# Top-k attention with a max-out MLP: the first sweep in seven groups of keys instead of eight

## The chip, the cores and the metric

The kernel runs on one core of one Trainium2 chip. The metric is device time in microseconds, the median of three runs. Five engines are named as the profile names them: PE (TensorE, its weight loads PEld), DVE (VectorE), ACT (ScalarE), POOL (GpSimd) and SP (SyncE, which issues the transfers).

## The reference

Eight batches of eight heads; 576 queries and 576 keys of 64 numbers each. Of each row of scores the 32 largest are kept, the rest are masked, then softmax and the product with the values. The heads are joined into 512 columns and go through a max-out MLP.

```python
scores = scale * np.matmul(q, k.transpose(0, 1, 3, 2))
kth = np.partition(scores, -top_k, axis=-1)[..., -top_k:-top_k + 1]
mask = scores >= kth
scores = np.where(mask, scores, -1000000000.0)
...
attn = attn / (np.sum(attn, axis=-1, keepdims=True) + 1e-09)
return np.matmul(attn, v).astype(np.float32)
...
h = np.maximum(np.maximum(x @ w1, x @ w2), x @ w3)
return (h @ w_out).astype(np.float32)
```

## The kernel before

**Tiles and units.** A tile is 128 queries (rows) of one head against all 576 keys. Two heads lie together, and a unit is mostly one pair of heads and two blocks of 128 queries, so four tiles; the last 64 queries of two pairs make a unit of two tiles. That is 80 units, ten to a batch, and 288 tiles. What follows happens per unit.

**Scores.** `qk` (L461, PE) multiplies queries and keys in two halves of 288 keys; `evac` (L469, ACT) moves each half from PSUM to the tile `ssb`.

**The search for the 32nd largest.** It has a rough and an exact step. `sweep` (L478, DVE) takes with MAX8 the eight largest, sorted, of each of eight groups of 72 keys: four groups after the first half of the scores has come, four after the second. The first four of each group (32 values, A) are negated by `negate` (L484, ACT) into `nA`; the last four (32 values, B) go to `pivot` piece 1 (L492, DVE), which keeps their eight largest in `b9`, behind a slot that holds a huge constant. Pieces 2 and 3 (L496, L502, L504) take the sixteen smallest of A in two MAX8 of `nA` with a MATCH_REPLACE8 between them; L498 gives the row's maximum. Piece 4 (L507) forms the minimum of A's (24-j)th largest and B's jth largest, for j = 0 to 7, and piece 5 (L509) the largest of these: the 24th largest of A and B together. This is the pivot. It is at most the true 24th largest of the row; its rank is 24 plus what the groups left out.

The exact step is `sign` (L517, ACT), which counts keys against the pivot, `window` (L522, POOL), which leaves the keys below the pivot positive, and `below` (L526, DVE), a MAX8 over all 576 that gives the next eight. `pick` (L537 to L542) chooses the 32nd by the count. This works while the pivot's rank is 24 to 32. `review` notes rows where it was not, and at the end a flag starts a second, slow pass over everything (the `tc.If(redo != 0)` block) if there is one.

**Softmax and values.** `mask` (L565, DVE), `expo` (L574, ACT), `inverse` (L589, DVE), `turn` (L620 to L625, PE transposes) and `turned` (L633, ACT), `values` (L650, PE), `scaled_x` (L667, DVE).

**MLP.** `layer` (L706, PE, three fp16 products for each of three weights), `largest` (L715, DVE, two of three; L713, ACT, the first), `high_h` and `low_h` (ACT, POOL), `layer2` (L766, PE). A batch's MLP needs all of its units. During the first batch VectorE also decodes the weights (L253 to L255).

**What sets the order.** Every engine works through its instructions in program order. `in_order` writes that order out: it lists the pieces of all units and the MLP, and picks, engine by engine, the piece that can start first by its own table of costs. Attention pieces are ranked by their unit plus a number from `OFFSETS`, within `LEAD` units of the lowest rank; `PATIENCE` says how long an engine may hold out for a piece of lower rank. The MLP is `fill`: PE takes it where no attention piece can start. So the costs and the tables decide where each instruction stands, on all engines.

Of the kernel before, what the change touches and what calls it, by code (L numbers as in the profile page):

```python
# [8 lines left out]
F32 = mybir.dt.float32  # L9
# [5 lines left out]
ALU = mybir.AluOpType  # L15
# [2 lines left out]
TOPK = 32  # L18
H_SCALE = 2.0 ** -12
CUT = 256  # L20
G = 8
GW = 72
NW = 9
SHRINK = 2.0 ** -61
BIG = 3.0e38
# [39 lines left out]
def in_order(pieces, fill):  # L65
# [72 lines left out]
DECODE_OUT = 1920.0  # L138
LOAD_JOB = 6500
SCORES = 960  # L140
PATIENCE = {'PE': 83.0, 'DVE': 164.4, 'ACT': 0.0, 'POOL': 81.9, 'SP': 0.0}


@with_exitstack
def kernel(ctx, tc, q, k, v, moe_w1, moe_w2, moe_w3, moe_w_out, out):
    nc = tc.nc
    B, NP, _, S = q.shape
    H, D = 2 * NP, q.shape[2] // 2
    P = 128
# [13 lines left out]
    sm = ctx.enter_context(tc.tile_pool(name="sm", bufs=3))  # L163
# [263 lines left out]
    b9s = [const.tile([P, 4, 9], F32, name=f"b9_{i}") for i in range(3)]  # L427
# [20 lines left out]
    def qk(n, g, i):  # L448


        b, hps, us = units[n]
        if n not in st:
            open_unit(n)
        s = ps_s.tile([P, 2, 512], F32, name="s")
        u = us[g]
        for x, hp in enumerate(hps):
            both = T_of[b, hp]
            c0, m, to = (u * P, P, s) if u < NU else (MAIN, 64, s[64 * x:64 * x + 64])
            for h in range(2):
                sl = slice(64 * h, 64 * h + 64)  # L460
                nc.tensor.matmul(to[:, h, :HALF], both[sl, 0, c0:c0 + m], both[sl, 1, i * HALF:(i + 1) * HALF], start=True, stop=True)  # L461
        st[n]["s"][g, i] = s

    def evac(n, g, i):
        d = st[n]
        if i == 0:
            t = d["both", g] = wk.tile([P, 2, S], F32, name="ssb", bufs=NSSB)
            d["ssb"] += [t[:, 0], t[:, 1]]
        nc.scalar.activation(d["both", g][:, :, i * HALF:(i + 1) * HALF], d["s"].pop((g, i))[:, :, :HALF], AF.Copy, scale=SCORE_SCALE)  # L469

    def sweep(n, g, i):

        d = st[n]
        if (g, i) == (0, 0):
            d["L"] = sm.tile([P, 4, G, 8], F32, name="L", bufs=NSM)
        for t in (2 * g, 2 * g + 1):
            for k in range(i * G // 2, (i + 1) * G // 2):
                nc.vector.max(d["L"][:, t, k, :], d["ssb"][t][:, k * GW:(k + 1) * GW])  # L478

    def negate(n):  # L480

        d = st[n]
        nA = d["nA"] = sm.tile([P, 4, G, 4], F32, name="nA", bufs=NSM)
        nc.scalar.activation(nA[:, :d["nt"]], d["L"][:, :d["nt"], :, 0:4], AF.Copy, scale=-1.0 / SHRINK)  # L484

    def pivot(n, piece):

        d = st[n]
        nt, L, nA = d["nt"], d["L"], d.get("nA")
        if piece == 1:  # L490
            for t in range(nt):
                nc.vector.max(b9s[n % 3][:, t, 1:9], L[:, t, :, 4:8])  # L492
        elif piece == 2:
            n8 = d["n8"] = sm.tile([P, 4, 2, 8], F32, name="n8", bufs=NSM)
            for t in range(nt):
# [330 lines left out]
    n = len(units)  # L826
# [10 lines left out]
    def attention(n):  # L837

        b, hps, us = units[n]
        nt = 2 * len(us)  # L840
        half = us[0] == NU
        gs = range(len(us))
        d = of[n] = {}
        p = lambda key, *a, **kw: d.setdefault(key, piece(*a, rank=(place_of[n], ("_" if b == 0 else "") + (key if isinstance(key, str) else "".join(map(str, key)))), **kw))
# [17 lines left out]
        swept = d["s", gs[-1], 1]
# [20 lines left out]
        for t in range(nt):  # L883
            g = t // 2
# [46 lines left out]
    def held(n, *key):  # L931
        return holders.setdefault((n, *key), [])
# [77 lines left out]
    with tc.If(redo != 0):  # L1010
        with tc.For_i(0, B, 1) as b:
# [79 lines left out]
```

## Time and profile before

| | us |
|---|---|
| median of three runs | 1258.01 (1257.69 to 1258.57) |
| the profiled execution | 1259.42 |
| its span, first to last instruction | 1257.6 |
| PE busy in the span | 1146.8 (91%) |
| DVE busy | 1146.7 (91%) |
| ACT busy | 1038.8 (83%) |
| POOL busy | 569.3 (45%) |
| PE weight loads busy | 776.2 (62%) |

How to read it: an engine's busy time is the union of its instructions, and two instructions in a row may overlap, since one starts before the last has left the engine. What an instruction costs its engine is therefore the distance from its start to the next one's, not its length. A busy share is an average over a startup, a long middle and a tail, which have different limits. The chain of waits is followed back from the last instruction; each step goes to what released it, or to the instruction before it.

### The profile page before, as it was taken

Reading aid. Unit: us, or ns where it says so; the run is one execution under the profiler, and the core shown is the slowest. Engines: PE = TensorE matmul, PEld = TensorE weight load, DVE = VectorE, ACT = ScalarE, POOL = GpSimd, SP = SyncE. Lnnn points to the kernel's source line nnn. Section 1 sums busy time; section 2 is a strip of 40 time slices with the busy share of each in tenths; the row PEclk is TensorE's granted clock in tenths of the full one; section 3 lists DMA queues with packets and bytes.
Section 4 is the critical chain, followed back from the end, with each engine's and each line's share of the span. In section 5 each row is a group of like instructions: output and inputs, shape, how many; then the busy total and the mean of one; then the engine's idle time right before and its main releaser. Section 6 shows DMA issues by size and latency. Waiting matters only on the chain.

```text
span 1257.6 us, 27583 instructions
## 1 busy us (share of the span) xinstructions
PE 1146.8 (91%) x8817; PEld 776.2 (62%) x8817; DVE 1146.7 (91%) x5728; ACT 1038.8 (83%) x2692; POOL 569.3 (45%) x503
## 2 busy tenths in 40 slices
PE   5275886999899999999999999999999999999998
PEld 2142653566576666766676666766677665767765
DVE  7999999999999999999999999999999999997121
ACT  6587888999989988999999989898899989897211
POOL 2444644654345544545555545445535454544111
PEclk8567986999999999999999999999999999999999
DMA  7141121202010102010101102020101000000000
GB/s 246 34 158 39 52 70 49 66 2 80 21 58 18 60 1 76 11 47 31 47 31 39 39 2 85 1 77 2 60 19 60 18 20 26 1 19 2 17 18 29
DMA packets 25754, 54.41 MB, mean 43 GB/s; under 512 B 2688, under 2 KB 2944, under 8 KB 25600
## 3 DMA queue, kind: packets, MB, share of 16 engines
q1 hardware_dynamic: 25296, 52.14, 12.6%
q8 instruction: 71, 1.16, 0.4%
q14 instruction: 83, 0.68, 0.2%
q10 hardware_dynamic: 304, 0.43, 0.1%
HBM read 43.12 MB, written 9.44 MB: 42 GB/s over the span
## 4 chain that ended last, share of the span: by engine, by line
DVE 49%; PE 39%; ACT 7%; issue 3%; POOL 1%; DMA 0%; ACTq 0%; DVEq 0%
PE m L706 19%; DVE L L478 13%; DVE ssb L565 9%; DVE Q L526 8%; PE m L766 5%; PE tr L625 5%; PE tr L650 5%; PE s L461 4%; DVE h L715 3%; DVE nR L502 2%; ACT w L517 2%; ACT pm L574 2%; DVE wall L254 1%; DVE n L504 1%; DVE n L496 1%
## 5 line engine op out<-in xcount | busy, mean ns | idle before, releaser
L522 POOL TENSOR_TENSOR w<-ssb,w 128x576 f32<-128x576 f32 x288 | 414.9, 1460 | 259.3 <-ACT w L517 257.0
L706 PE MATMUL m<-xh,wall 128*128 128x256 f16 (+1 forms) x2304 | 436.5, 287 | 4.8 <-DVE h L715 3.6
L706 PEld LDWEIGHTS <-wall 128*128 128x128 f16 x3456 | 338.0, 98 | 95.4 <-issue 15.9
L478 DVE MAX8 L<-ssb 128x8 f32<-128x72 f32 x2304 | 331.2, 218 | 6.8 <-ACT ssb L469 6.7
L706 PE MATMUL m<-xl,wall 128*128 128x320 f16 (+1 forms) x1152 | 330.7, 287 | 0.0
L574 ACT ACTIVATE pm<-ssb,nb 128x576 f32<-128x576 f32 x288 | 222.7, 775 | 42.4 <-DVE ssb L565 41.7
L565 DVE SCALAR_TENSOR_TENSOR ssb<-ssb,kth 128x576 f32<-128x576 f32 x288 | 241.7, 873 | 2.2
L517 ACT ACTIVATE w<-ssb,Q 128x576 f32<-128x576 f32 x288 | 223.2, 775 | 14.9 <-DVE Q L509 13.5
L633 ACT COPY pT<-tr 128x512 f32<-128x512 f32 (+1 forms) x432 | 215.1, 512 | 12.1 <-PE tr L622 6.6
L526 DVE MAX8 Q<-w 128x8 f32<-128x576 f32 x288 | 212.3, 747 | 1.3 <-POOL w L522 0.8
L625 PE MATMUL tr<-ident,pm 128*128 128x128 f32 x1152 | 183.0, 286 | 33.3 <-ACT pm L574 15.1
L461 PE MATMUL s<-qk 64*128 64x288 f32 (+1 forms) x1280 | 191.1, 451 | 16.6 <-ACT ssb L469 11.1
L469 ACT ACTIVATE ssb<-s 128x576 f32<-128x576 f32 x288 | 184.3, 650 | 10.0 <-PE s L461 9.7
L625 PEld LDWEIGHTS tr<-ident,pm 128*128 128x128 f32 x1152 | 130.2, 144 | 98.5 <-ACT pm L574 39.3
L650 PE MATMUL tr<-pT,vt 128*64 128x256 f32 (+1 forms) x1920 | 183.3, 340 | 0.1
L715 DVE SCALAR_TENSOR_TENSOR h<-m,rises,h 128x256 f32<-128x256 f32 (+1 forms) x192 | 97.2, 506 | 67.4 <-PE m L706 67.3
L650 PEld LDWEIGHTS tr<-pT,vt 128*64 128x64 f32 x1920 | 109.8, 140 | 69.1 <-issue 20.7
L721 POOL TENSOR_TENSOR hl<-h,hh 128x256 f16<-128x256 f32 (+1 forms) x96 | 72.7, 758 | 171.4 <-ACT hh L718 171.3
L461 PEld LDWEIGHTS s<-qk 64*128 64x128 f32 (+1 forms) x1280 | 99.9, 184 | 76.4 <-ACT ssb L469 28.2
L674 POOL TENSOR_TENSOR xl<-xs,xh 128x256 f16<-128x256 f32 (+1 forms) x80 | 55.1, 688 | 196.4 <-ACT xh L670 196.3
L766 PE MATMUL m<-wall,hh 128*128 128x512 f16 (+1 forms) x444 | 130.6, 377 | 3.2 <-ACT wall L318 1.2
L718 ACT CAST hh<-h 128x256 f16<-128x256 f32 (+1 forms) x96 | 41.5, 432 | 54.1 <-DVE h L715 53.4
(95 smaller groups left out, 1148.5 us busy)
## 6 DMA issues: line engine op xcount, KB each, us to landing
vt<-in_v_dram SPq DMA_DIRECT2D x32, 320.0 KB, 3.2
qk<-in_k_dram SPq DMA_DIRECT2D x34, 288.0 KB, 3.0
qk<-in_q_dram SPq DMA_DIRECT2D x33, 288.0 KB, 3.5
wall<-in_moe_w_dram SPq DMA_DIRECT2D x16, 512.0 KB, 6.0
out_dram<-ob SPq DMA_DIRECT2D x32, 256.0 KB, 2.0
wall<-in_moe_w_out_dram SPq DMA_DIRECT2D x3, 512.0 KB, 3.5
ssb<-in_moe_w_out_dram SPq DMA_DIRECT2D x3, 512.0 KB, 3.6
wall<-in_moe_w_dram SPq DMA_DIRECT2D x4, 256.0 KB, 5.9
```

Source lines behind the costliest of these rows:

```text
L461: nc.tensor.matmul(to[:, h, :HALF], both[sl, 0, c0:c0 + m], both[sl, 1, i * HALF:(i + 1) * HALF], start=True, stop=True)
L478: nc.vector.max(d["L"][:, t, k, :], d["ssb"][t][:, k * GW:(k + 1) * GW])
L517: nc.scalar.activation(d["w"][t], d["ssb"][t], AF.Sign, bias=d["Q"][:, t, 0:1], scale=-1.0, accum_out=d["cnt"][:, t:t + 1])
L522: nc.gpsimd.tensor_tensor(d["w"][t], d["ssb"][t], d["w"][t], ALU.mult)
L526: nc.vector.max(d["Q"][:, t, 1:NW], d["w"].pop(t))
L565: nc.vector.scalar_tensor_tensor(ss, ss, d["kth"][:, t:t + 1], ss, ALU.is_lt, ALU.subtract, accum_out=d["lost"][:, t:t + 1])
L574: nc.scalar.activation(d["pm", t // 2][:, t % 2], d["ssb"][t], AF.Exp, bias=d["nb"][:, t:t + 1], scale=-1.0 / SHRINK, accum_out=d["sums"][ ...
L625: nc.tensor.transpose(pt[:, j * P:(j + 1) * P], pm[:, i, 64 * i + j * P:64 * i + (j + 1) * P], ident)
L633: nc.scalar.copy(pT[:, 512 * i:512 * i + m] if i < 2 else pT[:, 8 * P:10 * P], pt[:, :m])
L650: nc.tensor.matmul(to, vt[:, block if i < 4 else 8 + h, :], keys, start=(i == 0), stop=(i == 4))
L706: nc.tensor.matmul(box["ps", i][:, :c1 - c0], a, bb[:, kc, c0:c1], start=(kc == 0 and k == 0), stop=(kc == KC - 1 and k == 2))
L766: nc.tensor.matmul(box["po"][:n, :ds.stop - ds.start], a[:, f, cs], columns_of(bb, ds), start=(f == 0 and k == 0), stop=(f == FC - 1 and k ...
```

## The change

The first sweep goes over seven groups of 82 or 83 keys (edges 0, 82, 164, 247, 329, 412, 494, 576). Three groups (up to key 247) are taken after the first half of the scores, four after the second, so a pair of tiles has 6 and then 8 MAX8, where it had 8 and 8. A and B have 28 values each. The 24th largest of A and B is now formed of nine pairs, j = 0 to 8: the slice `low` picks the 5th to the 13th of the sixteen smallest of A, and `b9` is used with all nine slots. The order's costs follow (890 and 1170 for the two halves, 1080 and 1080 before), and `LEAD`, `OFFSETS` and `PATIENCE` have new numbers, so that instructions stand elsewhere on all engines.

```diff
-G = 8
-GW = 72
+G = 7
+EDGES = (0, 82, 164, 247, 329, 412, 494, 576)
+FRONT = 3
...
-LEAD = 122.6
+LEAD = 121.4
...
-PATIENCE = {'PE': 83.0, 'DVE': 164.4, 'ACT': 0.0, 'POOL': 81.9, 'SP': 0.0}
+PATIENCE = {'PE': 102.7, 'DVE': 167.3, 'ACT': 0.0, 'POOL': 142.3, 'SP': 0.0}
...
-            for k in range(i * G // 2, (i + 1) * G // 2):
-                nc.vector.max(d["L"][:, t, k, :], d["ssb"][t][:, k * GW:(k + 1) * GW])
+            for k in range(FRONT, G) if i else range(FRONT):
+                nc.vector.max(d["L"][:, t, k, :], d["ssb"][t][:, EDGES[k]:EDGES[k + 1]])
...
-            z = d["z"] = sm.tile([P, 4, 8], F32, name="z", bufs=2)
-            nc.vector.scalar_tensor_tensor(z[:, :nt], d["n8"][:, :nt, 1], -SHRINK, b9s[n % 3][:, :nt, 0:8], ALU.mult, ALU.min)
+            z = d["z"] = sm.tile([P, 4, 9], F32, name="z", bufs=2)
+            low = d["n8"].rearrange("p t a b -> p t (a b)")[:, :nt, 4 * G - 24:4 * G - 15]
+            nc.vector.scalar_tensor_tensor(z[:, :nt], low, -SHRINK, b9s[n % 3][:, :nt], ALU.mult, ALU.min)
...
-                p(("s", g, i), "DVE", 1080, lambda g=g, i=i: sweep(n, g, i),
+                p(("s", g, i), "DVE", 1170 if i else 890, lambda g=g, i=i: sweep(n, g, i),
```

The line numbers of the changed kernel are one or two higher from here on (L478 is L479, L526 is L528, L650 is L652, L706 is L708).

**VectorE at the start of the program** (L is the tile of the group maxima, b the eight of B, nA the negated A, n the sixteen smallest; a row with a count stands for so many in a row). Before:

```order
L478 MAX L<-ssb 128x8 x32
L492 MAX b_0_98<-L 128x8 x4
L496 MAX n_188<-nA 128x8 x4
L498 TENSOR_REDUCE nb<-nA 128x4
L478 MAX L<-ssb 128x8 x8
L502 MATCH_REPLACE nR<-n_188,nA 128x32 x4
L504 MAX n_188<-nR 128x8 x4
```

The changed kernel, the same place:

```order
L479 MAX L<-ssb 128x8 x28
L493 MAX b_0_98<-L 128x8 x4
L479 MAX L<-ssb 128x8 x6
L497 MAX n_197<-nA 128x8 x4
L499 TENSOR_REDUCE nb<-nA 128x4
L503 MATCH_REPLACE nR<-n_197,nA 128x28 x4
L505 MAX n_197<-nR 128x8 x4
```

The first unit's sweep is 28 instructions, not 32; the next unit's first half, now 6, comes before the reads of `nA`, not after. MATCH_REPLACE8 is over 28 values.

**VectorE in the middle, in the fourth batch** (xs is the scaled output of a unit, kth the 32nd largest, h the MLP's running maximum). Before:

```order
L667 SCALAR_TENSOR_TENSOR xs<-tr,down_v,pT 128x128
L507 SCALAR_TENSOR_TENSOR z<-n_8852,b_1_99 128x32
L609 TENSOR_REDUCE bad<-lost 128x1
L610 TENSOR_REDUCE bad<-over 128x1
L509 TENSOR_REDUCE Q<-z 128x4
L478 MAX L<-ssb 128x8 x24
L526 MAX Q<-w 128x8
L478 MAX L<-ssb 128x8 x8
```

The changed kernel, the same unit of that batch:

```order
L509 SCALAR_TENSOR_TENSOR z<-n_8680,b_1_99 128x36
L567 SCALAR_TENSOR_TENSOR ssb,lost<-ssb,kth 128x576 x2
L669 SCALAR_TENSOR_TENSOR xs<-tr,down_v,pT 128x128
L604 TENSOR_TENSOR junk<-Q,kth 128x324
L606 TENSOR_REDUCE same<-junk 128x36
L511 TENSOR_REDUCE Q<-z 128x4
L479 MAX L<-ssb 128x8 x6
L611 TENSOR_REDUCE bad<-lost 128x1
L612 TENSOR_REDUCE bad<-over 128x1
L479 MAX L<-ssb 128x8 x14
```

Piece 4 of the pivot (z) now stands ahead of the unit's `xs` with two masks between, where it stood right behind it; the review (junk, same, bad) now starts behind `xs`; and the next sweeps are cut at other places.

**PE at the last products of attention with the values** (tr is the PSUM tile of transposes and values, vt the values, m the MLP's). Before:

```order
L706 MATMUL m<-xl,wall 128x320
L625 MATMUL tr<-ident,pm 128x128 x4
L620 MATMUL tr<-ident,pm 128x128
L622 MATMUL tr<-ident,rsw 128x128
L706 LDWEIGHTS wall
L706 MATMUL m<-xh,wall 128x320
```

The changed kernel, the same place:

```order
L708 MATMUL m<-xl,wall 128x320
L622 MATMUL tr<-ident,pm 128x128
L624 MATMUL tr<-ident,rsw 128x128
L708 LDWEIGHTS wall
L708 MATMUL m<-xh,wall 128x320
```

The mixed transposes (L620, L622; now L622, L624) come first here, and the four of L627 (L625 before) follow six MLP products later. Counted over PE's whole order, 282 MLP products of 320 columns stand behind the last product with the values before, and 270 now; the rest behind it is the same.

## Rows read from the trace of the kernel before

**Rows 1.** The page, part 1: busy time and share of each engine.

```profile
span 1257.6 us, 27583 instructions
PE 1146.8 (91%) x8817; PEld 776.2 (62%) x8817; DVE 1146.7 (91%) x5728; ACT 1038.8 (83%) x2692; POOL 569.3 (45%) x503
```

**Rows 2.** The page, part 2: busy tenths of 40 slices of 31.4 us.

```profile
PE   5275886999899999999999999999999999999998
DVE  7999999999999999999999999999999999997121
```

**Rows 3.** Busy us of engines per batch of values, startup first, tail last.

```profile
core 0: us, PE busy (x) PEld busy (x) DVE busy (x) ACT busy (x) POOL busy (x), PEclk, DMA share, GB/s
0.00:227.30 227.30, 145.24 (x912) 87.72 (x912) 214.61 (x960) 173.15 (x411) 101.72 (x87) 0.77 0.28 91
227.30:360.60 133.30, 125.68 (x980) 83.45 (x978) 131.11 (x680) 124.02 (x328) 65.36 (x55) 0.99 0.14 45
360.60:499.60 139.00, 135.80 (x1072) 91.68 (x1068) 137.50 (x717) 124.27 (x329) 67.34 (x58) 1.00 0.12 37
499.60:632.40 132.80, 130.57 (x1048) 89.65 (x1044) 131.43 (x681) 123.43 (x328) 65.15 (x58) 1.00 0.11 37
632.40:766.60 134.20, 132.87 (x1062) 91.03 (x1060) 132.81 (x701) 122.65 (x327) 66.87 (x59) 1.00 0.11 37
766.60:902.30 135.70, 131.46 (x1058) 91.63 (x1056) 133.90 (x690) 121.67 (x324) 65.46 (x58) 0.99 0.11 34
902.30:1036.30 134.00, 131.19 (x1064) 91.71 (x1062) 132.26 (x701) 121.98 (x323) 66.05 (x59) 1.00 0.10 34
1036.30:1162.30 126.00, 124.63 (x999) 86.54 (x996) 117.10 (x572) 109.07 (x291) 60.57 (x54) 1.00 0.04 12
1162.30:1257.60 95.30, 89.33 (x643) 62.76 (x643) 15.94 (x35) 18.52 (x37) 10.77 (x15) 0.99 0.06 21
```

**Rows 4.** Who waited for whom, 300 to 1150 us: total, times, longest.

```profile
ACT pm L574 <- DVE ssb L565: 36.5, 35, 3.6
DVE h L715 <- PE m L706: 2.8, 4, 1.0
```

**Rows 5.** The same, 1150 us to the end.

```profile
DVE h L715 <- PE m L706: 64.5, 29, 9.8
```

**Rows 6.** VectorE in order of time, first sweep: start, length, names, count.

```profile
7.35 4.40 DVE L478 MAX8 L<-ssb 128x8 f32<-128x72 f32 x32 [6.15 <-ACT ssb L469]
11.67 0.45 DVE L492 MAX8 b<-L 128x8 f32<-128x32 f32 x4
```

**Rows 7.** VectorE in order of time, steady state, the same columns.

```profile
642.40 1.17 DVE L478 MAX8 L<-ssb 128x8 f32<-128x72 f32 x8
643.48 1.40 DVE L526 MAX8 Q<-w 128x8 f32<-128x576 f32 x2
644.80 0.18 DVE L537 SCALAR_TENSOR_TENSOR oh<-spots,cnt 128x36 f32<-128x36 f32 x1
```

**Rows 8.** VectorE groups: shapes, count, busy us, mean ns, idle before.

```profile
line engine op names shapes xcount | busy us, mean ns | idle before us <-releasers
L478 DVE MAX8 L<-ssb 128x8 f32<-128x72 f32 x2304 | 331.2, 218 | 6.8 <-ACT ssb L469 6.7
L565 DVE SCALAR_TENSOR_TENSOR ssb<-ssb,kth 128x576 f32<-128x576 f32 x288 | 241.7, 873 | 2.2
```

**Rows 9.** The sweep's line alone in two stretches: length, VectorE busy, count.

```profile
0.00:227.30 227.30, 53.94 (x377) 0.77 0.28 91
227.30:1162.30 935.00, 277.30 (x1928) 1.00 0.10 34
```

**Rows 10.** The chain of waits in order of time, the tail.

```profile
1162.30 2.55 PE m L706 x18
...
1164.96 6.52 PE m L706 x48
1171.47 7.77 PE m L766 x36
```

More of the change, by code (lines that the diff above doesn't have):

```diff
@@ L38 @@
 LOCK_B = -103.0
-OFFSETS = {'C0': -22.23, 'C1': -0.68, 'C2': 16.29, 'C3': 22.05, 'D0': 0.65, 'D1': 1.18, 'D2': 13.19, 'D3': 21.59, 'E00': 0.38, 'E01': 4.0, 'E02': 8.06, 'E10': -7.03, 'E11': -5.47, 'E12': -6.74, 'N': -1.25, 'Pl': 16.72, 'R': 1.08, 'S': -0.87, 'T00': -45.95, 'T01': -24.59, 'T02': -5.36, 'T10': -53.3, 'T11': -22.41, 'T12': 19.1, 'U': -3.88, 'U0': -72.28, 'V': -20.52, 'V0': -5.15, 'Y': 1.32, 'Z': -34.63, '_E00': 0.1, '_E01': -53.2, '_E02': 11.13, '_E10': -7.53, '_E11': 7.46, '_E12': -93.53, '_N': 3.92, '_Pl': -15.8, '_T00': -80.59, '_T01': -65.28, '_T02': -75.59, '_T10': -76.62, '_T11': 15.54, '_T12': -1.54, '_Y': -6.93, '_Z': -27.25, '_d0': 3.3, '_d1': 3.35, '_e00': -78.77, '_e01': -96.54, '_e10': 1.02, '_e11': -65.33, '_g0': -51.8, '_g1': -100.97, '_g2': -84.62, '_g3': -4.5, '_h0': 4.78, '_h1': 6.26, '_h2': -79.13, '_k0': 4.08, '_k1': -64.87, '_k2': -10.46, '_k3': -39.33, '_m0': -71.19, '_m1': -17.42, '_m2': -11.19, '_m3': -4.1, '_p1': 4.08, '_p2': 2.51, '_p3': 5.06, '_p4': -83.77, '_p5': 5.82, '_q0': 3.47, '_q1': 5.12, '_r0': -103.78, '_r1': 1.33, '_s00': 2.75, '_s01': 4.33, '_s10': 5.6, '_s11': 5.27, '_v': 14.04, '_w0': 0.52, '_w1': 15.39, '_w2': -73.7, '_w3': -33.2, '_x0': 2.97, '_x1': 10.46, '_x2': 9.25, '_x3': 9.06, '_y': -22.79, '_z0': -15.82, '_z1': 9.51, 'd0': 10.91, 'd1': -28.85, 'e00': -2.76, 'e01': -0.16, 'e10': 5.37, 'e11': 5.58, 'g0': 2.04, 'g1': -4.67, 'g2': -0.74, 'g3': -8.38, 'h0': 4.53, 'h1': 8.33, 'h2': -0.67, 'k0': 1.09, 'k1': -16.36, 'k2': 1.43, 'k3': -17.57, 'm0': -11.23, 'm1': -7.14, 'm2': 4.41, 'm3': 5.68, 'p1': 8.78, 'p2': 5.97, 'p3': -14.32, 'p4': -9.47, 'p5': 7.14, 'q0': -1.54, 'q1': -1.52, 'r0': 0.62, 'r1': -9.75, 's00': 6.99, 's01': 5.11, 's10': 3.37, 's11': 8.54, 'v': 15.64, 'w0': -18.04, 'w1': 5.87, 'w2': -91.46, 'w3': -34.22, 'x0': 9.1, 'x1': -7.34, 'x2': 10.31, 'x3': 5.09, 'y': -14.22, 'z0': 12.43, 'z1': -0.29}
@@ new lines @@
+OFFSETS = {'C0': -52.17, 'C1': -8.39, 'C2': 20.78, 'C3': 25.27, 'D0': -3.67, 'D1': -11.41, 'D2': 13.52, 'D3': 19.44, 'E00': 2.87, 'E01': 11.42, 'E02': 6.06, 'E10': 0.9, 'E11': -11.49, 'E12': -11.11, 'N': -1.99, 'Pl': 15.81, 'R': -4.55, 'S': -1.11, 'T00': -39.4, 'T01': 6.68, 'T02': 4.12, 'T10': -16.91, 'T11': -58.21, 'T12': -34.79, 'U': -2.08, 'U0': -56.76, 'V': -7.97, 'V0': -9.28, 'Y': 5.88, 'Z': -40.2, '_E00': -10.31, '_E01': -91.05, '_E02': 11.79, '_E10': -23.47, '_E11': 2.33, '_E12': -47.42, '_N': 1.94, '_Pl': -81.73, '_T00': -92.24, '_T01': -34.72, '_T02': -44.33, '_T10': -97.46, '_T11': 2.04, '_T12': 12.8, '_Y': -50.99, '_Z': 19.87, '_d0': 5.5, '_d1': 5.05, '_e00': -44.64, '_e01': -71.18, '_e10': 2.42, '_e11': -110.26, '_g0': -96.72, '_g1': -14.95, '_g2': -72.95, '_g3': -62.07, '_h0': 1.1, '_h1': 5.66, '_h2': -0.41, '_k0': -17.15, '_k1': 3.94, '_k2': -0.91, '_k3': -7.49, '_m0': -88.87, '_m1': -31.01, '_m2': -15.05, '_m3': -8.52, '_p1': 3.44, '_p2': 3.99, '_p3': 5.81, '_p4': -99.85, '_p5': -1.15, '_q0': 2.1, '_q1': 2.6, '_r0': -99.96, '_r1': 4.2, '_s00': 0.06, '_s01': 4.56, '_s10': 5.6, '_s11': 5.0, '_v': -71.03, '_w0': 0.87, '_w1': -10.27, '_w2': -35.56, '_w3': -71.91, '_x0': 6.21, '_x1': 10.99, '_x2': 11.52, '_x3': 10.36, '_y': -41.36, '_z0': 5.46, '_z1': 7.87, 'd0': 10.69, 'd1': -23.64, 'e00': -2.83, 'e01': 0.2, 'e10': 7.32, 'e11': 3.19, 'g0': 1.79, 'g1': -19.4, 'g2': -5.26, 'g3': -5.82, 'h0': 4.52, 'h1': 7.81, 'h2': 0.29, 'k0': 1.47, 'k1': -17.01, 'k2': 0.27, 'k3': -15.47, 'm0': -11.36, 'm1': -11.59, 'm2': 5.31, 'm3': 3.36, 'p1': 8.95, 'p2': 6.8, 'p3': -17.32, 'p4': -9.76, 'p5': 7.91, 'q0': -1.88, 'q1': -0.73, 'r0': 1.72, 'r1': -10.69, 's00': 6.99, 's01': 8.26, 's10': 2.11, 's11': 6.68, 'v': 22.59, 'w0': 18.72, 'w1': 5.75, 'w2': -90.71, 'w3': -72.51, 'x0': 12.76, 'x1': 13.68, 'x2': 5.14, 'x3': 7.34, 'y': -12.07, 'z0': 4.63, 'z1': -5.29}
```

## The prediction

> **What bounds the kernel now.** I read the engines' busy times first: PE and VectorE are both at 91% of the span [rows 1], so neither is the bound by its average. The slices say why: VectorE is full from the second slice to the 36th and nearly idle in the last three, while PE is half idle in the first six and full from the eighth to the end [rows 2]. So there are three parts, which I cut at the last product with the values of each batch [rows 3]. In the **startup**, 0 to 227.3 us, VectorE is busy for 214.6 us and PE for 145.2: PE has little to do until the first batch is through, and VectorE (sweeps, pivots and the decoding of weights) sets the pace. In the **middle**, seven stretches of ten units, 227.3 to 1162.3 us, both are nearly full. PE's idle time per stretch is 7.6, 3.2, 2.2, 1.3, 4.2, 2.8 and 1.4 us (length less busy), 22.8 in all; VectorE's is 1.4 to 2.2 us until the last stretch, where its work runs out. In the **tail**, 95.3 us, PE does the MLP that is left over and VectorE waits for it (64.5 us of its 67 us of waits for PE lie there) [rows 5]; in the middle VectorE waits for PE's MLP products 2.8 us in all [rows 4].
>
> So the question is how much of a lighter VectorE the middle can use, since PE's work stays the same and has only 22.8 us of idle time there.
>
> **The price of a sweep instruction.** It is the distance from start to start, not the record. 32 MAX8 over 72 keys start at 7.35 and the next instruction at 11.67 us: 135 ns each [rows 6]; eight in the middle take from 642.40 to 643.48, again 135 ns, and two MAX8 over 576 keys from 643.48 to 644.80, 660 ns each [rows 7]. That is 1.042 ns per key (525 ns over 504 keys) and 60 ns that does not depend on the keys.
>
> A page would price it otherwise. The Trainium skill, "VectorE: DVE Perf Modes", section "The TRN2 errata — SBUF-src ops pay a fixed extra latency per instruction", gives 58 cycles plus the elements, and adds that the measured fixed term of a single operation is about 150 cycles, 156 ns; 288 instructions fewer would by that estimate save 45 us. The group's mean record, 218 ns [rows 8], does look like the larger term, but the spacing of 135 ns [rows 6] decides for the smaller.
>
> **The sweep.** 2304 instructions at 135 ns become 2016 over 82.3 keys on average, at 60 + 85.7 = 145.7 ns: 311.0 us become 293.7, 17.3 less. All 576 keys are still read, so this is just 288 times 60 ns.
>
> **The pivot.** The four instructions per tile that run over A or B (L492, L496, L502, L504) have 28 values in place of 32: 4 x 1.042 ns x 4 x 288 = 4.8 us less. The row maximum (L498) has an eighth less, 0.3 us; pieces 4 and 5 have nine pairs in place of eight, four elements per full unit in each, 0.6 us more. VectorE's work falls by 17.3 + 4.8 + 0.3 - 0.6 = **21.8 us**, 1.9% of its busy time. ScalarE's `negate` reads an eighth less, under 1 us in all, hidden: ScalarE has 9 to 14 us idle in every stretch [rows 3].
>
> **The other split, 6 and 8.** The part that must wait for the second half of the scores grows from 8 x 135 = 1.08 us to 8 x 145.7 = 1.17 us per pair of tiles. It would cost 0.09 us where VectorE waits for scores. It waits so for 6.7 us in the whole run, nearly all before the first sweep [rows 6, 8]; so I take nothing. If that cover went, 144 pairs would cost up to 13 us.
>
> **Nothing is added to PE**, POOL or the queues of SP; no wait is added. What POOL and ScalarE do per tile stays. What moves is the order, and it moves everywhere.
>
> **Startup.** 377 of the 2304 sweeps run there [rows 9], 3.6 us of the 21.8. But the new order fills some of it: counted in the orders, ahead of the tenth `xs` stand 384 sweeps before and 328 now (51.8 and 47.8 us), 44 of each pivot instruction (0.7 us less), three more MAX8 over 576 keys (2.0 us) and two more masks (at 0.84 us each at most, 241.7/288 [rows 8]). That is 4.0 + 0.7 - 2.0 - 1.7 = 1.0 us less. With VectorE setting the pace, I take 1 us; the bounds are 0 and 3.6. The other 20.8 us of VectorE's saving then fall in the middle, 3.0 us per stretch.
>
> **Tail.** In the changed order 270 products of 320 columns stand behind the last product with the values, 282 before; all else is equal. 48 of them take 6.52 us [rows 10], 136 ns each: 12 x 136 = 1.6 us less in the tail, and 1.6 us more for PE in the middle.
>
> **Middle, bounded from both sides.** If VectorE alone sets the pace, all 20.8 us come through. If PE does, a stretch can at best come down to the idle time of PE's fullest one, 1.3 us in 134 [rows 3]: the gains are the smaller of 3.0 and the idle time above 1.3, so 3.0, 1.9, 0.9, 0, 2.9, 1.5 and 0.1, together 10.3, less the 1.6 us of products that moved in: 8.7 us. Neither end is right alone. PE's idle time is understated, because products start every 136 ns [rows 10] while a record is longer than that, so that short waits between them lie under records; this speaks for more than 8.7. But PE's work hangs on VectorE through masks, exponentials and transposes (ScalarE waits 36.5 us for masks in the middle [rows 4]), and two engines that both want the whole time do not fit without loss. I take the mean of the ends, 14.8 us.
>
> **Sum.** 1.0 + 14.8 + 1.6 = 17.4 us less. The profiled execution took 1259.4 us (span 1257.6 and 1.8 around it) and would take 1242.0. The median of the runs is 1.4 below the profiled execution, so the forecast is **1240.6 us**, its own range 1237.5 to 1247.
>
> **Rival 1: VectorE alone sets the pace; PE has room.** All comes through: 1258.0 - 1.0 - 20.8 - 1.6 = **1234.6**. For it: VectorE waits almost never in the middle [rows 4], and PE's attention steps are taken ahead of the MLP. Against it: stretches with PE at 99% [rows 3], and the new order leaves no more MLP to the tail but less. The Trainium skill, "Perfetto Trace Analysis", section "Identifying the Most-Contended Engine", takes this side: matmul busy time is a bad measure of how full PE is, weight-load busy is a good one, and that is 62% here [rows 1]. The spacing of the products in the tail [rows 10] speaks against so much room. Chance 0.20.
>
> **Rival 2: PE takes over at once.** Only the two stretches in which PE idles above 4 us give their 3 us each, and the startup nothing: 5.9 us with tail and moved products cancelling, **1252**. For it: PE's 98 to 99% in the other five. Against it: the idle time under records. Chance 0.16 (1247 to 1255.5).
>
> **Rival 3: slower.** VectorE works in order and now reaches the MLP's maxima (L715) sooner than PE has the products. Each such wait holds up the sweeps and masks queued behind it; ScalarE's exponentials and PE's transposes wait for those, and PE fills in with MLP it would have needed later. What a bad arrangement of ten units costs shows in the second stretch: 139.0 us where the fourth takes 134.2, for the same ten units [rows 3]. Were all seven at 139.0, the middle would take 973 us, not 935: +38, against the whole saving of 23: 1258 + 38 - 23 = **1273**. It decides from (20.8 + 1.0 + 1.6)/7 = 3.3 us lost per stretch. Against it: 2.8 us of such waits in the middle now. Chance 0.06.
>
> **Rival 4: the change doesn't do what it says for a row.** The exact step works for a pivot of rank 24 to 32. Worked out on the host from the reference's inputs with seed 0, the largest rank of 36,864 rows is 30 with eight groups and 31 with seven (868 rows above rank 24, before 403). One row at 33 would start the slow pass over everything and more than double the time, over 2500 us. Chance 0.01.
>
> That gains and losses cancel to within 0.2% (2.5 us, about what a measurement of this kernel can tell from no change) has 0.05.
>
> **How the numbers follow.** Forecast 0.52, rival 1 0.20, rival 2 0.16, no change 0.05, rival 3 0.06, rival 4 0.01. Faster 0.52 + 0.20 + 0.16 = 0.88; same 0.05; slower 0.07. The range runs from 1232, rival 1 with 2.6 us of VectorE's own idle time in the middle taken too, to 1252, rival 2's value; outside lie the slower cases, no change, half of rival 2 and a little below, 0.2.
>
> **What would show each step.** Sweeps spaced at 145 to 146 ns and 17 us less busy on that line; MATCH_REPLACE8 and the short MAX8 4 ns closer; the last product with the values at about 1146 us and a tail of 93 to 94 us behind it; PE's idle time in the middle at 8 us or so. If VectorE's idle time in the middle grows by more than 6 us and its waits for L706 with it, PE has taken over; if PE's idle time stays near 22 us with the span 23 us shorter, rival 1 holds; longer waits of L715 in the middle and a longer span are rival 3. A spacing of sweeps other than 145.7 ns, or an odd start of a group costing extra, would make the first term wrong.

## The result

The changed kernel takes **1236.18 us** (median of four runs, 1235.86 to 1237.13) where the kernel before takes 1258.26. The ratio is 0.9826, with a 95% interval of 0.9811 to 0.9842: 22 us faster. The forecast was 1240.6 in a range of 1232 to 1252.

The page of the changed kernel, its span and part 1:

```profile
span 1234.3 us, 27367 instructions
PE 1139.7 (92%) x8817; PEld 779.0 (63%) x8817; DVE 1115.5 (90%) x5440; ACT 1032.7 (84%) x2692; POOL 568.0 (46%) x503
```

Against [rows 1] the span is 23.3 us shorter. VectorE is busy for 31.2 us less, more than the 21.8 that the instructions account for, and PE, which has the same work, for 7.1 us less. Both are worth following.

Busy time per stretch, cut as in [rows 3] at the last product with the values of each batch (length; then PE, PEld, DVE, ACT, POOL, PE's granted clock as a share of full speed, DMA share, GB/s):

```profile
0.00:227.70 227.70, 150.49 (x920) 93.26 (x920) 212.80 (x914) 176.68 (x422) 106.08 (x91) 0.76 0.28 91
227.70:354.60 126.90, 121.63 (x972) 81.13 (x970) 124.80 (x639) 118.15 (x318) 58.71 (x52) 1.00 0.14 47
354.60:493.10 138.50, 136.72 (x1096) 94.56 (x1092) 135.02 (x687) 126.60 (x338) 68.91 (x61) 1.00 0.11 38
493.10:621.90 128.80, 127.70 (x1030) 87.84 (x1026) 126.81 (x648) 121.39 (x323) 63.40 (x57) 1.00 0.12 38
621.90:752.90 131.00, 130.16 (x1055) 90.37 (x1053) 128.57 (x653) 119.71 (x320) 65.59 (x59) 1.00 0.11 36
752.90:888.80 135.90, 134.69 (x1091) 94.27 (x1089) 131.87 (x669) 124.19 (x331) 66.60 (x59) 1.00 0.12 38
888.80:1020.30 131.50, 130.96 (x1073) 92.12 (x1071) 129.54 (x666) 123.00 (x331) 66.52 (x59) 1.00 0.10 33
1020.30:1140.60 120.30, 119.48 (x969) 83.80 (x965) 110.22 (x536) 104.98 (x283) 61.40 (x53) 1.00 0.04 13
1140.60:1234.30 93.70, 87.87 (x637) 61.61 (x633) 15.92 (x35) 17.99 (x36) 10.76 (x15) 0.99 0.06 21
```

The startup takes 227.7 us (before 227.3), the middle 1140.6 - 227.7 = 912.9 (before 935.0), the tail 93.7 (before 95.3). So the whole gain but 1.6 us is in the middle, 22.1 us. PE's idle time per stretch (length less busy) is now 5.3, 1.8, 1.1, 0.8, 1.2, 0.5 and 0.8 us, 11.6 in all, where it was 22.8; VectorE's total in the middle rose from 18.9 to 26.1 (2.1, 3.5, 2.0, 2.4, 4.0, 2.0, 10.1). Who waits for whom, 300 to 1130 us (total, times, longest):

```profile
ACT pm L576 <- DVE ssb L567: 33.7, 36, 2.5
DVE h L717 <- PE m L708: 2.3, 5, 0.8
```

VectorE's waits for MLP products are as short as before [rows 4]; ScalarE's waits for masks are a little shorter.

VectorE in order of time in the steady state (start, length, names, count), and three of its groups (count | busy us, mean ns | idle before):

```profile
650.64 1.25 DVE L479 MAX8 L<-ssb 128x8 f32<-128x82 f32 x8
651.80 0.74 DVE L528 MAX8 Q<-w 128x8 f32<-128x576 f32 x1
```

```profile
L479 DVE MAX8 L<-ssb 128x8 f32<-128x82 f32 (+1 forms) x2016 | 311.2, 228 | 5.7 <-ACT ssb L470 5.7
L567 DVE SCALAR_TENSOR_TENSOR ssb<-ssb,kth 128x576 f32<-128x576 f32 x288 | 232.2, 837 | 2.1
L503 DVE MATCH_REPLACE8 nR<-n,nA 128x28 f32<-128x28 f32 x288 | 46.3, 171 | 0.0
```

Eight sweeps go from 650.64 to 651.80, 145 ns each where they were 135 [rows 7]; the record of one is 228 ns where it was 218 [rows 8]. The masks (L567) are the surprise: the same 288 instructions are busy for 232.2 us and took 241.7 before [rows 8].

### The profile page after: what moved, and what is told of

The parts are those of the page before. It is cut to its first block, busy times and chain, and to the rows that moved or that the text cites. A ratio compares the mean times of both kernels' runs of the same rounds, so it can differ in the third digit from the quotient of the medians.

```text
span 1234.3 us, 27367 instructions
## 1 busy us (share of the span) xinstructions
PE 1139.7 (92%) x8817; PEld 779.0 (63%) x8817; DVE 1115.5 (90%) x5440; ACT 1032.7 (84%) x2692; POOL 568.0 (46%) x503
## 4 chain that ended last, share of the span: by engine, by line
PE 33%; DVE 30%; ACT 8%; POOL 3%; issue 2%; DVEq 0%; ACTq 0%
PE m L708 16%; DVE L L479 7%; DVE ssb L567 7%; DVE Q L528 6%; PE m L768 5%; PE tr L652 4%; PE tr L627 4%; PE s L462 3%; POOL w L524 3%; ACT pm L576 3%; DVE h L717 2%; ACT w L519 2%; DVE nR L503 2%; ACT pT L635 1%; DVE n L505 1%
## 5 line engine op out<-in xcount | busy, mean ns | idle before, releaser
L524 POOL TENSOR_TENSOR w<-ssb,w 128x576 f32<-128x576 f32 x288 | 410.1, 1445 | 314.9 <-ACT w L519 310.5
L708 PE MATMUL m<-xh,wall 128*128 128x256 f16 (+1 forms) x2304 | 435.0, 286 | 1.7 <-DVE h L717 1.6
L708 PEld LDWEIGHTS <-wall 128*128 128x128 f16 x3456 | 337.1, 98 | 89.0 <-issue 10.7
L708 PE MATMUL m<-xl,wall 128*128 128x320 f16 (+1 forms) x1152 | 329.8, 286 | 0.0
L479 DVE MAX8 L<-ssb 128x8 f32<-128x82 f32 (+1 forms) x2016 | 311.2, 228 | 5.7 <-ACT ssb L470 5.7
L567 DVE SCALAR_TENSOR_TENSOR ssb<-ssb,kth 128x576 f32<-128x576 f32 x288 | 232.2, 837 | 2.1
L528 DVE MAX8 Q<-w 128x8 f32<-128x576 f32 x288 | 213.1, 749 | 6.1 <-POOL w L524 4.7
L627 PE MATMUL tr<-ident,pm 128*128 128x128 f32 x1152 | 182.9, 285 | 29.1 <-ACT pm L576 19.2
L462 PE MATMUL s<-qk 64*128 64x288 f32 (+1 forms) x1280 | 194.2, 454 | 14.1 <-ACT ssb L470 9.0
L627 PEld LDWEIGHTS tr<-ident,pm 128*128 128x128 f32 x1152 | 130.7, 144 | 91.6 <-ACT pm L576 34.9
L652 PE MATMUL tr<-pT,vt 128*64 128x256 f32 (+1 forms) x1920 | 183.6, 342 | 3.7 <-ACT pT L635 3.7
L652 PEld LDWEIGHTS tr<-pT,vt 128*64 128x64 f32 x1920 | 111.9, 142 | 72.0 <-issue 19.2
L723 POOL TENSOR_TENSOR hl<-h,hh 128x256 f16<-128x256 f32 (+1 forms) x96 | 76.7, 799 | 165.7 <-ACT hh L720 165.3
L768 PE MATMUL m<-wall,hl 128*128 128x512 f16 (+1 forms) x222 | 83.1, 374 | 0.0
```

The costliest lines, as they stand in the source:

```text
L479: nc.vector.max(d["L"][:, t, k, :], d["ssb"][t][:, EDGES[k]:EDGES[k + 1]])
L524: nc.gpsimd.tensor_tensor(d["w"][t], d["ssb"][t], d["w"][t], ALU.mult)
L528: nc.vector.max(d["Q"][:, t, 1:NW], d["w"].pop(t))
L567: nc.vector.scalar_tensor_tensor(ss, ss, d["kth"][:, t:t + 1], ss, ALU.is_lt, ALU.subtract, accum_out=d["lost"][:, t:t + 1])
L627: nc.tensor.transpose(pt[:, j * P:(j + 1) * P], pm[:, i, 64 * i + j * P:64 * i + (j + 1) * P], ident)
L652: nc.tensor.matmul(to, vt[:, block if i < 4 else 8 + h, :], keys, start=(i == 0), stop=(i == 4))
```

## The experiments

The order of a kernel hangs on its tables alone, so the two halves of the change can be taken apart: the groups in the old order, and the new order with the old groups. In every experiment but e10 each instruction stands where it does in the kernel named, apart from those added or left out. Times are medians. The kernel before took 1256.6 to 1257.4 us in the sets of the experiments and 1258.26 in that of the changed kernel, so a difference between two sets is known to 1 or 2 us only; the ratios compare within a set.

| | groups | order | added or left out | us | ratio to before (95%) |
|---|---|---|---|---|---|
| before | 8 | old | | 1257 | 1 |
| e1 | 7 | old | | 1241.99 | 0.9879 (0.9863 to 0.9896) |
| e2 | 8 | new | | 1252.98 | 0.9963 (0.9949 to 0.9977) |
| after | 7 | new | | 1236.18 | 0.9826 (0.9811 to 0.9842) |
| e3 | 7 | new | VectorE +22 us | 1256.99 | 0.9998 (0.9989 to 1.0008) |
| e6 | 8 | old | VectorE +22 us | 1280.76 | 1.0187 (1.0164 to 1.0210) |
| e5 | 8 | old | PE +31 us | 1263.96 | 1.0057 (1.0040 to 1.0073) |
| e12 | 8 | new | PE +31 us | 1259.35 | 1.0021 (1.0010 to 1.0031) |
| e11 | 7 | old | PE +31 us | 1255.01 | 0.9989 (0.9980 to 0.9999) |
| e4 | 7 | new | PE +31 us | 1254.70 | 0.9981 (0.9971 to 0.9990) |
| e7 | 7 | new | PE -35 us | 1229.77 | 0.9783 (0.9766 to 0.9799) |
| e8 | 6 | new | | 1228.71 | 0.9775 (0.9759 to 0.9791) |
| e9 | 6 | new | PE +31 us | 1247.25 | 0.9923 (0.9907 to 0.9940) |
| e10 | 6 | its own | | 1240.17 | 0.9857 (0.9841 to 0.9874) |

### Groups or order: e1 and e2

e1 is the changed kernel with the tables and the sweep's cost of the kernel before:

```diff
-LEAD = 121.4
+LEAD = 122.6
...
-                p(("s", g, i), "DVE", 1170 if i else 890, lambda g=g, i=i: sweep(n, g, i),
+                p(("s", g, i), "DVE", 1080, lambda g=g, i=i: sweep(n, g, i),
```

(`OFFSETS` and `PATIENCE` likewise.) e2 is the opposite, the kernel before with the three tables and the costs of the changed one.

> Seven groups, 28 values and nine pairs, but every instruction stands where it stood in the kernel before (its OFFSETS, LEAD, PATIENCE and the sweep costs of 1080). Theory A, VectorE set the pace in the middle and its 21.8 us come through at once: 1236 to 1240 us, nearly all of the gain of 22 us. Theory B, much of the gain is the new order (masks that stall less, PE's waits): 1246 to 1252 us here. Theory C, PE was the bound in half of the stretches: the same as B, but then PE's idle time in the middle falls to 12 us or less.

> Eight groups of 72 as before, but in the order of the changed kernel (its OFFSETS, LEAD, PATIENCE and sweep costs); the sweep's instructions stand in the same places, eight and eight where six and eight stood. Theory A, the order gives nothing by itself: 1256 to 1261 us. Theory B, the order carries half of the gain: 1244 to 1250 us.

Measured: the groups alone give 15.1 us, the order alone 4.1 (4.7 by the ratio), both 22. Theory A was nearer for e1 and missed by 2 us; for e2 it was wrong by 3 and B by 3. Theory C has its sign, PE's idle time at 12 us or less (11.4, below), but not its time. About seven tenths of the gain are the groups. The stretches tell more, with care: each is of one execution, and that of the kernel before (1259.42) is slower than its median, that of e1 (1241.03) faster, so that their spans differ by 18.4 us where the medians differ by 15.1. The middle of the kernel before, as one stretch, then e1 and e2 in their startup, middle and tail:

```profile
227.30:1162.30 935.00, 912.20 (x7267) 625.69 (x7264) 916.11 (x4735) 847.09 (x2244) 456.80 (x401) 1.00 0.10 34
```

```profile
0.00:227.30 227.30, 142.54 (x912) 86.26 (x912) 215.17 (x912) 173.00 (x411) 101.42 (x87) 0.79 0.28 91
227.30:1143.90 916.60, 905.16 (x7266) 624.39 (x7262) 895.02 (x4495) 842.65 (x2244) 456.05 (x401) 1.00 0.11 35
1143.90:1239.20 95.30, 89.51 (x649) 62.81 (x645) 15.93 (x35) 18.53 (x37) 10.77 (x15) 0.98 0.06 21
```

```profile
0.00:231.90 231.90, 150.49 (x920) 93.72 (x920) 217.93 (x960) 177.63 (x422) 105.50 (x91) 0.76 0.26 89
231.90:1156.60 924.70, 907.15 (x7270) 622.60 (x7266) 903.05 (x4734) 841.33 (x2235) 452.01 (x398) 1.00 0.10 34
1156.60:1250.20 93.60, 87.91 (x639) 61.74 (x634) 15.94 (x35) 17.99 (x36) 10.79 (x15) 1.00 0.06 21
```

In the old order the groups take 18.4 us off the middle (935.0 to 916.6), and VectorE was made 21.8 - 3.6 = 18.2 us lighter there by the prediction's figures. By these two executions all of it came through; by the medians the kernel as a whole gained 15.1 of the 21.8 us. PE's idle time fell by half (22.8 to 11.4 us), and PE's busy time by 7.0 us with the same products. That second part was idle time hidden under records. How it can hide, the MLP's products of 320 columns in the kernel before show (count | busy us, mean ns | idle before):

```profile
L706 PE MATMUL m<-xh,wall 128*128 128x320 f16 x1152 | 239.1, 300 | 0.8 <-DVE h L715 0.7
```

They start 136 ns apart where nothing holds them [rows 10], and a record lasts 300 ns, so a wait of up to 164 ns between two of them shows as busy. Added up over the MLP's products and the 128-column transposes of the middle (distance to the next start above the least one, as far as the record reaches), such waits are 36.7 us before, 31.1 in e1 and 28.8 in the changed kernel.

The new order takes 10.3 us off the middle (924.7) and 1.7 off the tail, but its startup is 4.6 us longer (231.9): it puts three more MAX8 over 576 keys and two more masks ahead of the tenth `xs`, as the prediction counted. With seven groups 4.2 of these come back (227.7). VectorE is busy for 13.1 us less in the middle of e2 (903.1, before 916.1). Some 4 us of that is the work that has only moved into the startup; the rest is, by the trace, in the masks. The line of the masks in e1 (old order), then in e2 (new order):

```profile
L567 DVE SCALAR_TENSOR_TENSOR ssb<-ssb,kth 128x576 f32<-128x576 f32 x288 | 240.3, 867 | 2.2
```

```profile
L565 DVE SCALAR_TENSOR_TENSOR ssb<-ssb,kth 128x576 f32<-128x576 f32 x288 | 233.6, 841 | 2.1
```

240.3 us busy in the old order and 233.6 in the new; before it was 241.7 [rows 8], after 232.2. The mask instruction is the same in all four. What makes some of them long is told at the end.

### How full is VectorE: e3 and e6

One more MAX8 over 16 keys per tile, into a spare tile, in the changed kernel (e3) and in the kernel before (e6):

```diff
+    spare8 = const.tile([P, 8], F32, name="spare8")
...
         for t in (2 * g, 2 * g + 1):
+            if i:
+                nc.vector.max(spare8, d["ssb"][t][:, 0:16])
```

> The changed kernel, same order, with one more MAX8 over 16 keys per tile into a spare tile: 288 x (60 + 17) = 22 us more on VectorE, 2.8 per batch, at the places where the sweep saved its time. Theory A, VectorE still sets the pace: 1254 to 1259 us, that is 0.85 to 1 us per us added. Theory D, PE has taken over after the change: 1240 to 1248 us, under 0.5 us per us.

> The kernel before, same order, with the MAX8 over 16 keys per tile of e3: 22 us more on VectorE. Theory A: 0.94 us per us or more, as VectorE set the pace even more than after: 1278 to 1281 us. Rival E: the same 0.94 as after the change, 1278. Under 1270 us VectorE would not have been the pace of the kernel before.

The 22 us cost 20.8 in the changed kernel (0.94 per us) and 23.9 in the kernel before (1.08). By the ratios, within a set, they are 21.6 and 23.5, and the interval of e6 alone runs from 20.6 to 26.4, so the two can't be told apart. Theory A held both times: what is added to VectorE is paid about in full. It is not paid evenly: the startup, with 46 or 48 of the 288 instructions (3.6 us), is 5.4 us longer in e3 and 5.9 in e6, and the middle, with 18.6 us of them, 16.3 and 14.6 by these executions. e3 also undoes the change's gain to the microsecond, 1256.99 beside 1257.08 for the kernel before in the same set, though it has the new order.

### How full is PE: e4, e5, e11, e12

Two more transposes per pair of tiles, into an unused part of the PSUM tile:

```diff
+            for j in (2, 3):
+                nc.tensor.transpose(pt[:, j * P:(j + 1) * P], pm.rearrange("p t s -> p (t s)")[:, 4 * P:5 * P], ident)
             nc.tensor.transpose(pt[:, P:2 * P], d["rsw"].pop(g).rearrange("p h d -> p (h d)"), ident)
```

> The changed kernel, same order, with two more transposes per pair of tiles into an unused part of the PSUM tile: 288 x 109 ns = 31 us more on PE, 3.9 per batch; the startup has room for its eighth. Theory D, PE has taken over: 1258 to 1264 us, 0.8 to 1 us per us outside the startup. Theory A, VectorE alone sets the pace and PE has room: under 1246 us, less than a third.

> The kernel before, same order, with the two more transposes per pair of tiles of e4: 31 us more on PE. Theory A (before the change VectorE set the pace and PE had room, after it less): clearly less than the 18.5 us that the same load cost the changed kernel, 1262 to 1270 us. Rival E, the room on PE was the same before and after (PE's share of the pace did not change): 1274 to 1278 us.

The 31 us cost 18.5 us in the changed kernel and 7.1 in the kernel before. So before the change PE had room for three quarters of them, and after it for four tenths: theory A held for e5 at its lower end, and for e4 neither A (under 1246) nor D (1258 and more) was right. The middle of e5, then of e4:

```profile
227.30:1167.30 940.00, 929.17 (x7516) 654.93 (x7514) 917.59 (x4726) 850.34 (x2241) 456.41 (x401) 1.00 0.10 34
```

```profile
229.60:1159.90 930.30, 922.92 (x7520) 653.84 (x7518) 894.89 (x4492) 844.57 (x2235) 451.82 (x398) 1.00 0.10 34
```

e5 takes the load in 5.0 us (940.0 beside 935.0), e4 in 17.4 (930.3 beside 912.9). PE's busy time in e5 rose by 17 us for 27 us of transposes: again 10 us went in under records.

Whether this is the lighter VectorE or the new order, e11 (seven groups, old order) and e12 (eight groups, new order) tell, with the same edit:

> Seven groups in the order of before (e1, 1242 us), with the two more transposes per pair of tiles. The load cost 7 us with eight groups in the old order (e5), 18.5 with seven in the new (e4) and 18.5 with six in the new (e9). Theory G, PE's part in the pace comes from VectorE being lighter: about 15 to 20 us here, 1257 to 1262. Theory H, it is a matter of the order alone: 6 to 9 us, 1248 to 1251.

> Eight groups in the order of the changed kernel (e2, 1253 us), with the two more transposes per pair of tiles. Theory G: VectorE is as heavy as before, so 6 to 9 us, 1259 to 1262. Theory H: the new order makes the kernel feel PE, 16 to 20 us, 1269 to 1273.

With eight groups the load costs 7.1 us in the old order and 6.4 in the new; with seven 13.0 and 18.5. Theory G held for eight groups and theory H fell, but e11's 13.0 lies below the 15 to 20 that G gave. The lighter VectorE adds 5.9 us to the cost in the old order and 12.1 in the new; the order adds nothing with eight groups and 5.5 us with seven. So neither does it alone.

### The other side: less PE, six groups

e7 leaves one of twelve fp16 products out of each accumulation of the MLP's first layer:

```diff
-                for k, (a, bb) in enumerate(((high, xh), (low, xh), (high, xl))):
+                for k, (a, bb) in enumerate(((high, xh), (low, xh), (high, xl))[:2 if kc == KC - 1 else 3]):
...
-                                     stop=(kc == KC - 1 and k == 2))
+                                     stop=(kc == KC - 1 and k == 1))
```

> The changed kernel, same order, with one of the twelve fp16 products of every MLP accumulation left out (the low half of x with the last quarter of the rows), so the MLP's result lacks that part: 288 products, 35 us less on PE, about 5 of them in the tail. If PE takes part in the pace of the middle, as the 18.5 us of e4 for 31 say: 1236 - 5 - 10 to 18 = 1213 to 1221 us. If VectorE alone sets the pace after the change: the tail's 5 us alone, 1229 to 1232 us.

1229.77, 6.4 us less. Middle and tail:

```profile
229.60:1140.00 910.40, 886.71 (x7041) 598.93 (x7037) 886.57 (x4492) 837.12 (x2236) 451.00 (x398) 1.00 0.11 35
1140.00:1228.60 88.60, 82.84 (x598) 57.68 (x594) 15.93 (x35) 18.00 (x36) 10.77 (x15) 1.00 0.06 22
```

5.1 us are the shorter tail (88.6). The middle, 910.4, is 2.5 us shorter for some 30 us less PE work, and the startup 1.9 longer (229.6). So the guess drawn from e4 was wrong: that more PE work is paid at 0.6 does not mean that less of it is paid back. It is not PE's amount of work that holds the middle here; VectorE, busy for 886.6 of the 910.4 us as in the changed kernel, has more part in it, though e8 (below) shows that it does not hold it alone.

e8 goes one step further on the change's own way, six groups of 96 in the changed kernel's order:

```diff
-G = 7
-EDGES = (0, 82, 164, 247, 329, 412, 494, 576)
+G = 6
+EDGES = (0, 96, 192, 288, 384, 480, 576)
```

> Six groups of 96 in the order of the changed kernel (24 values in A and in B, nine pairs): another 288 MAX8 fewer, 17 us, and 5 us on the pivot, so VectorE 22 us lighter again; nothing else changes. Theory A as before the change (VectorE sets the pace): 1236 - 20 = 1216 us. Theory D (PE near its end after the change, its idle time in the middle was halved): the second step brings much less than the first, 1224 to 1232 us.

1228.71, 7.5 us less than seven groups, as theory D said; it is 28.2 us (2.3%) below the kernel before and faster than the changed one. Its middle:

```profile
227.40:1134.10 906.70, 898.30 (x7268) 624.58 (x7266) 873.04 (x4250) 837.02 (x2236) 451.40 (x398) 1.00 0.11 35
```

VectorE is 13.8 us less busy there than with seven groups (873.0, 886.8), the middle only 6.2 us shorter; VectorE's idle time rose to 33.7 us, PE's fell to 8.4. This is where the gain of a lighter VectorE falls off: the first 21.8 us gave 15.1 in the old order and 16.8 in the new (e2 to after), the second 7.5.

e9 adds the transposes of e4 to it:

> Six groups in the changed kernel's order (e8), with the two more transposes per pair of tiles of e4 and e5: 31 us more on PE, 27 of them outside the startup. The same load cost 7 us with eight groups in the old order and 18.5 with seven. Theory D (with six groups PE sets the pace): 24 to 31 us, 1253 to 1260 us. Rival F (ScalarE or the waits between the engines set it, PE is no more the bound than with seven): 16 to 21 us, 1245 to 1250 us.

1247.25, again 18.5 us more. Theory D wanted 24 or more and fell; rival F's number came out. PE is not more of a bound with six groups than with seven. What does hold the middle of e8 was not settled: PE has 8.4 us idle there, ScalarE 69.7 and VectorE 33.7, and no experiment took ScalarE's share away.

e10 gives the planner the six groups' own price, so that it writes a new order, with the other tables kept:

```diff
-                p(("s", g, i), "DVE", 1170 if i else 890, lambda g=g, i=i: sweep(n, g, i),
+                p(("s", g, i), "DVE", 960, lambda g=g, i=i: sweep(n, g, i),
```

> Six groups with the sweep's own price (960 and 960) in the table of costs, the other tables as in the changed kernel, so that the order is written out anew around the lighter sweep. If the 7.5 us that six groups gave in the order made for seven were held down by that order: 1220 to 1226 us. If the engines are simply full: within 2 us of e8's 1228.7, or above it, since the offsets were not chosen for it.

1240.17, 11.5 us worse than e8 with the same instructions. Its middle and tail:

```profile
225.50:1127.60 902.10, 888.47 (x7147) 609.97 (x7143) 871.32 (x4246) 833.98 (x2233) 447.87 (x397) 1.00 0.11 35
1127.60:1238.60 111.00, 105.05 (x765) 73.96 (x761) 19.25 (x41) 21.47 (x43) 13.93 (x19) 0.99 0.05 18
```

Its middle is the shortest of all, 902.1 us, but 111.0 us of MLP are left for the tail, 17 more than in e8. Here a true price in the table was worth nothing, since the offsets had been chosen around another.

## Why the prediction was right, and where it was off

**The sign, the range and the place were right.** The sum gave 17.4 us, 22 came. 1236.18 lies just below the forecast's own range of 1237.5 to 1247; the stated range held it because it reached down over rival 1.

**The sweep and the pivot: right.** The spacing was put at 145.7 ns and is 145; the sweeps' busy time fell by 20.0 us (331.2 to 311.2 us), where the count of the prediction gave 17.3. MATCH_REPLACE8 fell from 47.6 to 46.3, 1.3 us, put at 1.2. That the smaller fixed term is the price, 60 ns and not 156, is thereby shown: at 156 ns the sweeps alone would have saved 45 us.

**The split 6 and 8: right**, no wait of the sweep for scores appeared in the middle.

**The tail: right**, 1.6 us (95.3 to 93.7).

**The startup: near, by luck of two terms.** The prediction took 1 us less; it is 0.4 more. The new order costs 4.6 us there (e2), which the prediction's count put at 3.7; the groups give back 4.2 in that order. In the old order they give back nothing (e1: 227.3 as before), where the count gave 3.6. Executions with the same VectorE work differ by some 2 us there (229.6 in e4 and e7, 227.7 in the changed kernel), so these are rough figures. In e1 VectorE's busy time in the startup did not fall (215.2, before 214.6): the sweeps are busy for 2.7 us less, but the masks for 1.5 more (34.5, before 33.0), some of it waits for POOL (below), and the decoding of the weights for 1.2 more; why that, is open. VectorE set the pace of the startup, but its work there did not shrink by what was taken out.

**The middle: this step failed, in size.** It was the mean of two ends, 8.7 if PE sets the pace and 20.8 if VectorE does, 14.8; it measured 22.1. The lower end rested on the idle time of PE's fullest stretch, 1.3 us, as a floor. It was none: six of the seven stretches now lie at 0.5 to 1.8, and PE's busy time itself fell by 11 us (912.2 to 901.3) for the same work. The prediction named the reason, idle time under records, and did not let it decide. And the upper end was no bound either: it took the new order to be neutral, while e2 shows it worth 4.1 us in all and 10.3 in the middle, of which some 4 had only moved into the startup. What each half gives does not add up exactly: 18.4 + 10.3 = 28.7 us in the middle by single executions, where 22.1 came, but 15.1 + 4.1 = 19.2 us by the medians, where 21 to 22 came. Whether they help or hinder each other is open.

**Rival 1** gave 1234.6 and was nearest, in part by chance: in the old order the groups alone gave 15.1 us and not its 21.8, and the order, which it put at nothing but the tail, made up the rest. Of the signs given beforehand neither side's came whole: the span is 23.3 us shorter, but PE's idle time did not stay near 22 us (11.6), and VectorE's idle time in the middle grew by 7.2 us, but not its waits for products. Its mechanism, that VectorE sets the pace and PE has room, is shown for the kernel before: a microsecond on VectorE cost 1.08 (e6), one on PE 0.23 (e5). The rule of the Trainium skill that stood beside it ("Perfetto Trace Analysis", "Identifying the Most-Contended Engine") was borne out there: PE, 91% busy with weight loads at 62%, had room. After the change the weight loads are at 63% and the room is mostly gone (0.59 per us, e4), so that share alone did not tell the two apart.

**Rival 2** (PE takes over at once) fell with e1 and e7. **Rival 3** (slower, through L715): VectorE's waits for products in the middle are 2.3 us, before 2.8; it did not happen. **Rival 4**: one pass, no second one in the trace. One reading of the rows was off, with nothing resting on it: ScalarE's idle time per stretch is 9.3 to 16.9 us, not 9 to 14.

## What to carry to other kernels

Price an instruction by the distance from its start to the next one's, and ask of two engines that are both 91% busy what a microsecond added to each would cost: a cheap load on one engine at a time, with the order held fixed, answers it; here the answer held upward only (e4 and e7). A matmul's busy time hides idle time under its records, so the least idle stretch of such a trace is no floor. When a change carries a new order with it, run the two halves crosswise, since the order may carry a good part of the gain.

## What the runs showed of the hardware

**A mask waits for the end of a POOL instruction that is running when it comes up.** In the kernel before, 22 of the 288 masks have records over 1 us; 21 of them started while POOL was in an instruction, and each of these ended 613 to 620 ns after that instruction did. Of the 260 with records up to 0.85 us, 8 started so, and in these the POOL instruction had at most 0.22 us to go. VectorE in the startup of the kernel before, and POOL's row beside it:

```profile
68.78 0.80 DVE L565 SCALAR_TENSOR_TENSOR ssb<-ssb,kth 128x576 f32<-128x576 f32 x1
69.51 1.96 DVE L565 SCALAR_TENSOR_TENSOR ssb<-ssb,kth 128x576 f32<-128x576 f32 x1
71.40 1.95 DVE L565 SCALAR_TENSOR_TENSOR ssb<-ssb,kth 128x576 f32<-128x576 f32 x1
68.83 5.77 POOL L522 TENSOR_TENSOR w<-ssb,w 128x576 f32<-128x576 f32 x3 [1.86 <-ACT w L517]
```

The mask at 68.78 us comes just before POOL's first instruction of three (68.83) and takes 0.80; the next two each wait one POOL instruction out, 1.96 and 1.95 us. The same place in e1, where VectorE comes 0.8 us sooner:

```profile
68.00 2.00 DVE L567 SCALAR_TENSOR_TENSOR ssb<-ssb,kth 128x576 f32<-128x576 f32 x1
69.93 1.95 DVE L567 SCALAR_TENSOR_TENSOR ssb<-ssb,kth 128x576 f32<-128x576 f32 x1
71.81 1.94 DVE L567 SCALAR_TENSOR_TENSOR ssb<-ssb,kth 128x576 f32<-128x576 f32 x1
67.97 5.16 POOL L524 TENSOR_TENSOR w<-ssb,w 128x576 f32<-128x576 f32 x3 [1.85 <-ACT w L519]
```

The first mask now starts 0.03 us after POOL (67.97 and 68.00) and takes 2.00 us: the lead of 0.8 us is gone, and VectorE stands 0.4 us later than before. This is a part of why the startup of e1 came out as long as before. In the changed kernel 12 masks have such records, in e2 13, in e1 21. Over the 0.815 us of a plain mask these records hold 16.5 us in the kernel before, 15.2 in e1, 8.1 in e2 and 6.8 in the changed kernel: the new order's doing, and about all of the 9.5 us by which the masks' busy time fell. The Trainium skill, "GPSIMD Engine Reference", section "1. Specifications", says that GpSimd shares its interfaces to SBUF with VectorE and contends with its instructions that have two inputs in SBUF, as the mask has; the trace agrees, and shows that the wait lasts to the end of the instruction. That this is what the new order gains by was read from the traces and not tried by a run of its own.
